# Starting x tile 0 and wk chunk 0 alone on two DMA queues, holding back the other loads, and turning the gate column with a full-height matmul

## The chip, the cores and the metric

The kernel runs on one core of one Trainium2 chip. The metric is the time of one execution in device microseconds (us). Most executions of a kernel agree within some tenths of a per cent, so a kernel is given by the median of several. The profile of an execution spans about 1.3 us less than its time.

Five engines matter. PE is the matrix engine (PEld is its weight load), DVE, ACT and POOL are the vector, the scalar and the GpSimd engine, and SP here only issues transfers. Loads are issued from the queues of SP and ACT (SPq and ACTq) and carried out by 16 DMA engines.

## The reference, cut to what matters

The kernel computes a linear-attention block and a gated feed-forward block on the same input and mixes them with a per-row gate. Only the very beginning matters here: the K and Q projections of the first two of sixteen row tiles of x, and the gate column.

```python
# x: (1, 2048, 640) bf16; wqkv: (640, 1920); gate_w: (640,)
g   = sigmoid((x * gate_w).sum(-1, keepdims=True))
qkv = x @ wqkv                    # q, k, v; 32 heads of 20
pq, pk = phi(q), phi(k)           # phi(t) = where(t > 0, t + 1, exp(t)) + 1e-6
a   = linear_attention(pq, pk, v) @ wo
b   = (gelu(x @ w_gate) * (x @ w_up)) @ w_down
out = g * a + (1 - g) * b
```

## The kernel before

The contraction dimension of 640 is cut into five chunks of 128. `T` transposes a tile of x on PE, `KM(n, ks)` adds the K projection of tile n over the chunks ks, as a 512-wide and a 128-wide matmul for each chunk, and `QM` does the same for Q. `gate_w` becomes column 640 of the Q weights, so that the Q projection also yields the gate; for that it has to be turned from a row into a column. `warm` runs filler matmuls on constants, whose result nobody reads: they are meant to keep PE busy while it waits for data, so that its clock rises early. In the profile below, PE starts a wide matmul every 0.43 us at first (called the cold pace here) and works at twice that pace (warm) from 6.16 us on.

The loads of the opening, in order of issue (`touch` is a small load whose data nobody uses):

```python
P.op("act", lambda e: e.dma_start(touch[0:16, 0:4], A_wqkv[0:128:8, 640:644]), ...)
load_x(0)              # SP queue; each of these is 160 KB
load_wk(0)             # SP
load_x(1, "act")       # ACT
load_wk(1)             # SP
load_wk(3)             # SP
# ... (an activation that loads the Exp table)
load_wk(2, "act")
load_wk(4, "act")
dma_in(gw_sb[0:5, :], gate_w.rearrange("(k p) -> k p", p=128), [r_gw], eng="act")
load_wq(0, 2)          # SP, 320 KB
load_wq(2, KC, "act")  # 480 KB
# ... DMA transposes of tiles 2 to 15, once wk chunk 4 has landed; then all other loads
```

The matmuls of the opening:

```python
def gate_col():
    P.op("pe", lambda e: e.transpose(psb[:, 7, 0:5], gw_sb[0:5, :], ident[0:5, 0:5]), ...)
    P.op("dve", lambda e: e.tensor_copy(wq[:, :, 640:641],
                                        psb[:, 7, 0:5].rearrange("p (k o) -> p k o", o=1)), ...)

warm(5, 512)
warm(1, 128)
T(0, [0], 7)
T(0, [1, 2, 3, 4], 6)
warm(6, 128)
KM(0, [0])
T(1, [0], 7)
T(1, [1, 2, 3, 4], 6)
warm(3, 128)
KM(1, [0])
for k in (1, 3):
    KM(0, [k])
    KM(1, [k])
gate_col()
for k in (2, 4):
    KM(0, [k])
    KM(1, [k])
# ... QM(2), QM(3): the Q projections of tiles 0 and 1; then KQ(i) for tiles 2 to 15; then the rest
```

PE takes these strictly in this order. If one of them waits for a load, everything behind it waits too.

Of the kernel before, what the change touches and what calls it, by code (L numbers as in the profile page):

```python
# [7 lines left out]
BF16 = mybir.dt.bfloat16  # L8
# [152 lines left out]
def bass_gated_mix__linear_attn_block__geglu_ffn__prompt_kernel(  # L161
# [17 lines left out]
    def take(n):  # L179
        nonlocal off  # L180
        o = off
        off += (n + 15) // 16 * 16
        return o
# [35 lines left out]
    O_G = take(32)  # L219
    O_OMG = take(32)  # L220
    O_GW = take(128)
    O_TOUCH = take(16)
    TOTAL = off

    omg_dram = nc.dram_tensor("omg_row", (S,), F32).ap()
# [3 lines left out]
    with (  # L229
# [8 lines left out]
        with contextlib.ExitStack() as stack:  # L238
            dma_sems = [stack.enter_context(nc.semaphore("s_in%d" % i)) for i in range(n_dma_in)]

            P = _Plan(["pe", "act", "dve", "pool", "sp"])
# [9 lines left out]
            def new_dma_key():  # L251
                k = "in%d" % dma_next[0]
                dma_next[0] += 1
                return k

            def v16(o, n):
                return pool[:, o:o + n]
# [5 lines left out]
            psb = ps[:].bitcast(BF16)  # L263


            x_aug = v16(R_XN, NT * XW).rearrange("p (i w) -> p i w", i=NT)
# [4 lines left out]
            wk = wkq[:, :, 0:640]  # L271
            wq = wkq[:, :, 640:1281]
# [23 lines left out]
            ident = v16(O_IDENT, 128)  # L296
# [6 lines left out]
            gg = v32(O_G, 16)  # L303
            omg = v32(O_OMG, 16)
            gw_sb = v16(O_GW, 128)
            touch = v16(O_TOUCH, 16)


            bank = [P.res("bank%d" % b, excl=True) for b in range(8)]
            r_xn = [P.sb("xn%d" % i, R_XN + i * XW, R_XN + (i + 1) * XW) for i in range(NT)]  # L310
# [4 lines left out]
            r_wk = [P.sb("wk%d" % k, R_WK + k * WW, R_WK + k * WW + 640) for k in range(KC)]  # L315
# [27 lines left out]
            r_gw = P.res("gw")  # L343

            def dma_in(dst, src, writes, reads=(), eng="sp"):
                P.op(eng, lambda e, dst=dst, src=src: e.dma_start(dst, src),
                     reads=reads, writes=writes, dma=new_dma_key())



            def load_x(i, eng):
                dma_in(x_aug[:, i, 0:640], A_x[0, i * 128:(i + 1) * 128, :], [r_xn[i]], eng=eng)

            def load_wk(k, eng):
                dma_in(wk[:, k, :], A_wqkv[k * 128:(k + 1) * 128, 640:1280], [r_wk[k]], eng=eng)


            def load_x(i, eng="sp"):
                dma_in(x_aug[:, i, 0:640], A_x[0, i * 128:(i + 1) * 128, :], [r_xn[i]], eng=eng)

            def load_wk(k, eng="sp"):
                dma_in(wk[:, k, :], A_wqkv[k * 128:(k + 1) * 128, 640:1280], [r_wk[k]], eng=eng)

            def load_wq(k0, k1, eng="sp"):
                dma_in(wq[:, k0:k1, 0:640],
                       A_wqkv[k0 * 128:k1 * 128, 0:640].rearrange("(k p) w -> p k w", p=128),
                       r_wq[k0:k1], eng=eng)


            P.op("act", lambda e: e.dma_start(touch[0:16, 0:4], A_wqkv[0:128:8, 640:644]),  # L370
                 writes=[P.res("touch")], dma=new_dma_key())
            load_x(0)
            load_wk(0)
            load_x(1, "act")
            load_wk(1)
            load_wk(3)

            zero = nc.const_aps.tensor(0.0, (128, 1), F32)
            P.op("act", lambda e: e.activation(eg[:, 0:1], zero, ACT.Exp), writes=[r_eg[0]])
            load_wk(2, "act")  # L380
            load_wk(4, "act")
            dma_in(gw_sb[0:5, :], gate_w.rearrange("(k p) -> k p", p=128), [r_gw], eng="act")
            load_wq(0, 2)
            load_wq(2, KC, "act")
# [15 lines left out]
            for c in range(NHC):  # L400
# [9 lines left out]
                 reads=[r_ones], writes=[r_ident])  # L410

            def late_constants():
                P.op("pool", lambda e: e.memset(x_aug[:, :, 640:641], 1.0), writes=[r_xone])
                P.op("pool", lambda e: e.memset(mask, 1.0), writes=[r_mask])
                for lo, hi, base, pat in ((0, 600, 0, [[0, 5], [20, 6], [0, 20]]),
# [5 lines left out]
                    P.op("pool", lambda e, lo=lo, hi=hi, base=base, pat=pat: e.affine_select(  # L421
                        mask[:, lo:hi], mask[:, lo:hi], pat, ALU.is_ge, 0.0, base=base + 19,
                        channel_multiplier=-1), reads=[r_mask], writes=[r_mask])

            one_l = nc.const_aps.tensor(1.0, (128, 128), BF16)
            one_r = nc.const_aps.tensor(1.0, (128, 512), BF16)

            def warm(count, n):
                def fn(e):
                    last = None  # L430
                    for w in range(count):
                        last = e.matmul(ps[:, 4, 0:n], one_l, one_r[:, 0:n], start=True, stop=True)  # L432
                    return last
                P.op("pe", fn, writes=[bank[4]])


            SLOTS = [(0, 1), (2, 3), (4, 5), (6, 7)]
# [1 line left out]
            def slot(n):  # L439
                return SLOTS[n % 4]  # L440

            def T(i, ks, tb):
                def fn(e):
                    last = None
                    for n, k in enumerate(ks):
                        last = e.transpose(psb[:, tb, n * 128:(n + 1) * 128],
                                           x_aug[:, i, k * 128:(k + 1) * 128], ident)
                    return last
                P.op("pe", fn, reads=[r_xn[i], r_ident], writes=[bank[tb]])
                P.op("dve", lambda e: e.tensor_copy(  # L450
                    xT[:, ks[0]:ks[-1] + 1, i * 128:(i + 1) * 128],
                    psb[:, tb, 0:len(ks) * 128].rearrange("p (k s) -> p k s", k=len(ks))),
                    reads=[bank[tb]], writes=[r_xTa[i] if ks[0] == 0 else r_xT[i]])
# [4 lines left out]
            def KM(n, ks):  # L458
                i = seq[n][1]
                b0, b1 = slot(n)  # L460

                def fn(e):
                    last = None
                    for k in ks:
                        lhs = xT[:, k, i * 128:(i + 1) * 128]
                        e.matmul(ps[:, b0, :], lhs, wk[:, k, 0:512], start=(k == 0), stop=(k == KC - 1))  # L466
                        last = e.matmul(ps[:, b1, 0:128], lhs, wk[:, k, 512:640],
                                        start=(k == 0), stop=(k == KC - 1))
                    return last
                P.op("pe", fn, reads=[r_xTa[i] if i < NXN and ks == [0] else r_xT[i]] + [r_wk[k] for k in ks],  # L470
                     writes=[bank[b0], bank[b1]])
# [35 lines left out]
                    reads=[bank[b0], bank[b1], r_e[m]], writes=[r_dst])  # L507

            def gate_col():
                P.op("pe", lambda e: e.transpose(psb[:, 7, 0:5], gw_sb[0:5, :], ident[0:5, 0:5]),  # L510
                     reads=[r_gw, r_ident], writes=[bank[7]])
                P.op("dve", lambda e: e.tensor_copy(wq[:, :, 640:641],
                                                    psb[:, 7, 0:5].rearrange("p (k o) -> p k o", o=1)),
                     reads=[bank[7]], writes=[r_gcol])


            ALLK = list(range(KC))
            warm(5, 512)
            warm(1, 128)
            T(0, [0], 7)  # L520
            T(0, [1, 2, 3, 4], 6)
            warm(6, 128)
            KM(0, [0])
            T(1, [0], 7)
            T(1, [1, 2, 3, 4], 6)
            warm(3, 128)
            KM(1, [0])
            for k in (1, 3):
                KM(0, [k])
                KM(1, [k])  # L530
            gate_col()
            for k in (2, 4):
                KM(0, [k])
                KM(1, [k])
            for n in range(4):
                if n == 2:
                    for k in range(3):
# [42 lines left out]
            for i in range(2, NT):  # L580
                KQ(i)
                if i == 4:
                    late_constants()
            P.op("dve", lambda e: e.tensor_scalar(gg, eg, 0.5, 0.5, ALU.mult, ALU.add),
                 reads=r_eg, writes=[r_g])
            P.op("dve", lambda e: e.tensor_scalar(omg, eg, -0.5, 0.5, ALU.mult, ALU.add),
                 reads=r_eg, writes=[r_omg])
            P.op("sp", lambda e: e.dma_start(omg_dram.rearrange("(i p) -> p i", p=128), omg,
                                             allow_slow_non_contiguous=True),
                 reads=[r_omg], writes=[r_od], dma=new_dma_key())  # L590
# [19 lines left out]
            def ME(g):  # L610
# [17 lines left out]
                for c in cs:  # L628
# [10 lines left out]
                 reads=r_z5, writes=[r_zd], dma=new_dma_key())  # L639
# [310 lines left out]
```

## Time and profile before

| | us |
|---|---|
| time, median of the first 3 executions (range) | 274.76 (274.43 to 275.19) |
| PE busy, of a span of 273.4 | 269.3 |
| first transposes of tile 0 | 3.10 |
| first K projection matmul (tile 0) | 4.38 |
| transposes of tile 1 | 4.87 |
| first Q projection matmul | 8.54 |

From the page of the profile, its summary line, busy times (share of the span, number of instructions) and the chain of work that ended last:

```profile
span 273.4 us, 3515 instructions
...
PE 269.3 (98%) x1385; PEld 130.8 (48%) x1412; DVE 138.9 (51%) x233; ACT 79.1 (29%) x137; POOL 36.2 (13%) x36
...
PE 97%; DVE 1%; issue 1%; ACT 1%; DVEq 0%; ACTq 0%
...
```

PE bounds the kernel. Fillers count as busy, so the busy share does not tell what the opening is worth; the time at which the first Q matmul starts does.

From the timeline of the first 9 us (start in us, duration in us, engine, source line, operation, operands, number of merged instructions; in brackets the idle time before it and what ended that). L432 is a filler, L446 a transpose of x, L466 and L467 the wide and narrow K matmul, L510 the gate column, L481 a Q matmul:

```profile
...
start us, us, engine line op out<-in xcount [idle before <-releaser]
...
0.80 0.40 SPq L346 DMA_DIRECT2D pool<-in_A_x_dram  x1
...
0.84 2.40 PE L432 MATMUL ps<-const-bfloat16-1.0 128*128 128x512 bf16 x6 [0.84 <-PEq L935]
...
1.24 0.45 ACTq L346 DMA_DIRECT2D pool<-in_A_x_dram  x1
1.26 1.83 SPq L346 DMA_DIRECT2D pool<-in_A_wqkv_dram  x4
...
3.10 0.72 PE L446 MATMUL ps<-pool 128*128 128x128 bf16 x5
...
4.38 0.59 PE L466 MATMUL ps<-pool 128*128 128x512 bf16 x1
...
4.87 0.74 PE L446 MATMUL ps<-pool 128*128 128x128 bf16 x5
...
5.41 0.53 PE L432 MATMUL ps<-const-bfloat16-1.0 128*128 128x128 bf16 x3
...
7.19 0.22 PE L467 MATMUL ps<-pool 128*128 128x128 bf16 x1
...
7.34 0.17 PE L510 MATMUL ps<-pool 5*128 5x5 bf16 x1
...
7.45 0.39 PE L466 MATMUL ps<-pool 128*128 128x512 bf16 x1
...
8.54 0.38 PE L481 MATMUL ps<-pool 128*128 128x512 bf16 x1
...
```

Tile 0 was issued at 0.80 us and its transposes start at 3.10, just as the six fillers end. Tile 1 was issued at 1.24 and its transposes start at 4.87, with no idle time in front. A wide and a narrow matmul take about 0.5 us together at the cold pace (4.38 to 4.87) and 0.27 at the warm one (the two pairs between 8.00 and 8.54); the first wide matmul at the warm pace starts at 6.16. Around the gate column, the pair at 7.45 comes 0.20 us later than the narrow matmul at 7.19 and its 0.05 us would have allowed.

Two more views: first, the table of windows, here two stretches of it. The last figure of a line is what the 16 DMA engines moved:

```profile
...
core 0: us, PE busy (x) PEld busy (x) DVE busy (x) ACT busy (x) POOL busy (x), PEclk, DMA share, GB/s
...
3.10:4.60 1.50, 1.50 (x14) 1.23 (x13) 0.65 (x2) 0.12 (x1) 1.30 (x3) 1.00 1.02 360
4.60:6.10 1.50, 1.50 (x11) 1.11 (x10) 0.65 (x2) 0.00 (x0) 0.00 (x0) 1.00 1.01 337
...
```

Second, the list of DMA issues in a short window, with the time from issue to landing. This is the load of x tile 1:

```profile
...
issues: line engine op xcount, KB each, median us to landing
pool<-in_A_x_dram ACTq DMA_DIRECT2D x1, 160.0 KB, 3.2
```

It was issued at 1.24 us and took 3.2 us, so it landed at about 4.4.

### The profile page before, as it was taken

To read this page: it belongs to the slowest core of one execution; us is meant where nothing else is said; L and a number is where in the kernel's file an instruction comes from. 1 tells how busy PE (TensorE), PEld (TensorE's weight loads), DVE (VectorE), ACT (ScalarE), POOL (GpSimd) and SP (SyncE) were. 2 spreads that over 40 slices of the span, in tenths; PEclk is the share of its full clock that TensorE was granted. 3 is DMA by queue.
4 is the path that set the end of the run, shared out by engine and by line. 5 is a ranking of instruction groups with operands and counts; after the bars stand their busy time and mean duration, and the time that the engine had idled before them with its cause. 6 is when DMAs were issued, how large, how long until landed. Compare 5 with 4: busy or idle time off the path is not lost.

```text
span 273.4 us, 3515 instructions
## 1 busy us (share of the span) xinstructions
PE 269.3 (98%) x1385; PEld 130.8 (48%) x1412; DVE 138.9 (51%) x233; ACT 79.1 (29%) x137; POOL 36.2 (13%) x36
## 2 busy tenths in 40 slices
PE   8999999999999999999999999999999999999997
PEld 5555555555445444444444444444444444444444
DVE  1688989610334334999999999534100132222232
ACT  2455555210521453223222223224566100000000
POOL 5000000000000401242332422000000240007000
DMA  7876999511140111612121421390000023111311
GB/s 224 177 106 123 353 401 382 111 26 24 27 48 4 66 52 48 189 38 48 25 48 28 46 48 26 58 314 15 1 0 2 0 58 97 39 38 37 100 38 58
DMA packets 43599, 24.10 MB, mean 88 GB/s; under 512 B 32831, under 2 KB 42047, under 8 KB 43455
## 3 DMA queue, kind: packets, MB, share of 16 engines
q1 hardware_dynamic: 42709, 22.89, 32.2%
q10 hardware_dynamic: 874, 0.98, 1.0%
q8 instruction: 11, 0.18, 0.3%
q14 instruction: 5, 0.04, 0.0%
HBM read 14.16 MB, written 2.63 MB: 61 GB/s over the span
## 4 chain that ended last, share of the span: by engine, by line
PE 97%; DVE 1%; issue 1%; ACT 1%; DVEq 0%; ACTq 0%
PE ps L692 41%; PE ps L885 16%; PE ps L553 12%; PE ps L807 6%; PE ps L602 6%; PE ps L859 4%; PE ps L604 2%; PE ps L670 2%; PE ps L820 2%; PE ps L432 1%; PE ps L466 1%; PE ps L840 1%; PE ps L481 1%; PE ps L713 1%; DVE pool L572 1%
## 5 line engine op out<-in xcount | busy, mean ns | idle before, releaser
L692 PE MATMUL ps<-pool 128*128 128x512 bf16 x510 | 113.0, 379 | 0.5
L692 PEld LDWEIGHTS ps<-pool 128*128 128x128 bf16 x520 | 50.5, 98 | 59.9
L700 DVE TENSOR_TENSOR pool<-ps,pool 128x512 bf16<-128x512 f32 x52 | 35.8, 688 | 33.3 <-PE ps L692 30.2
L698 ACT ACTIVATE pool<-ps 128x512 f32<-128x512 f32 x52 | 31.0, 597 | 72.4 <-PE ps L692 72.4
L885 PE MATMUL ps<-pool 128*128 128x512 bf16 (+2 forms) x217 | 45.4, 366 | 0.2
L746 POOL TENSOR_TENSOR pool<-pool 128x640 f32<-128x640 bf16 x16 | 22.5, 1408 | 138.6 <-DMA pool<-z_row 86.3
L553 PE MATMUL ps<-pool 128*128 128x512 bf16 (+1 forms) x206 | 37.9, 343 | 0.2
L885 PEld LDWEIGHTS ps<-pool 128*128 128x128 bf16 x221 | 21.0, 98 | 24.2 <-issue 0.6
L891 DVE SCALAR_TENSOR_TENSOR pool<-ps,pool 128x512 bf16<-128x512 f32 (+2 forms) x17 | 12.2, 720 | 33.7 <-PE ps L885 33.6
L553 PEld LDWEIGHTS ps<-pool 128*128 128x128 bf16 x210 | 20.5, 98 | 17.5
L572 DVE SCALAR_TENSOR_TENSOR pool<-ps,pool 128x128 bf16<-128x128 f32 (+2 forms) x42 | 25.3, 603 | 2.4
L563 ACT ACTIVATE pool<-ps 128x640 bf16<-128x640 f32 x28 | 19.7, 703 | 18.2 <-DVE pool L572 10.9
L754 DVE TENSOR_TENSOR pool<-pool 128x640 bf16<-128x640 bf16 x16 | 23.1, 1442 | 0.6
L602 PE MATMUL ps<-pool 128*128 128x512 bf16 x77 | 21.4, 379 | 0.0
L864 DVE TENSOR_TENSOR pool<-ps,pool 128x512 f32<-128x512 f32 x4 | 2.8, 692 | 31.0 <-PE ps L859 31.0
L807 PE MATMUL ps<-pool 128*128 128x512 bf16 x80 | 17.9, 379 | 0.0
L604 PE MATMUL ps<-pool 128*128 128x129 bf16 x80 | 17.6, 220 | 0.2
L866 POOL TENSOR_TENSOR pool<-pool 128x512 f32<-128x512 f32 x4 | 5.1, 1264 | 75.7 <-DVE pool L864 75.7
L748 DVE TENSOR_REDUCE pool<-pool 128x32 f32<-128x640 f32 x16 | 12.9, 809 | 0.0
L811 ACT ACTIVATE pool<-ps,pool 128x512 f32<-128x512 f32 x16 | 11.0, 687 | 6.6 <-PE ps L807 6.6
L807 PEld LDWEIGHTS ps<-pool 128*128 128x128 bf16 x80 | 7.8, 98 | 9.4
L602 PEld LDWEIGHTS ps<-pool 128*128 128x128 bf16 x80 | 7.8, 98 | 9.3
(66 smaller groups left out, 130.8 us busy)
## 6 DMA issues: line engine op xcount, KB each, us to landing
out_dram<-pool SPq DMA_DIRECT2D x19, 128.0 KB, 1.8
pool<-in_B_w_gate_dram SPq DMA_DIRECT2D x1, 2080.0 KB, 13.4
pool<-in_B_w_up_dram SPq DMA_DIRECT2D x1, 2080.0 KB, 19.1
pool<-in_A_x_dram SPq DMA_DIRECT2D x1, 1280.0 KB, 8.8
pool<-in_B_w_down_dram SPq DMA_DIRECT2D x1, 1120.0 KB, 7.3
pool<-omg_row SPq DMA_DIRECT2D x1, 1024.0 KB, 5.0
pool<-in_A_x_dram SPq DMA_DIRECT2D x1, 960.0 KB, 5.9
pool<-in_A_wo_dram SPq DMA_DIRECT2D x6, 160.0 KB, 10.4
```

The source lines that it names most:

```text
L553: last = e.matmul(ps[:, b + p, 0:c1 - c0], xT[:, k, i * 128:(i + 1) * 128], wkq[:, k, c0:c1], start=(k == 0), stop=(k == KC - 1))
L563: P.op("act", lambda e: e.activation(e_buf[m], ps_flat[:, o:o + 640], ACT.Exp), reads=banks, writes=[r_e[m]])
L572: P.op("dve", lambda e, c0=c0, c1=c1: e.scalar_tensor_tensor(dst[:, c0:c1], ps_flat[:, o + c0:o + c1], 1.0 + EPS, e_buf[m][:, c0:c1], ALU. ...
L602: e.matmul(ps[:, bs[n], :], lhs, x_aug[:, i, 0:512], start=(i == 0), stop=(i == NT - 1))
L604: last = e.matmul(ps[:, bt, n * 129:(n + 1) * 129], lhs, x_aug[:, i, 512:641], start=(i == 0 and n == 0), stop=(i == NT - 1), skip_group_c ...
L692: last = e.matmul(ps[:, b, :], w[:, k, fc * 128:(fc + 1) * 128], xT[:, k, j * 512:(j + 1) * 512], start=(k == 0), stop=(k == KC - 1))
L698: P.op("act", lambda e: e.activation(ge[n], ps[:, gb, :], ACT.Gelu_apprx_tanh), reads=[bank[gb]], writes=[r_ge[n]])
L700: P.op("dve", lambda e: e.tensor_tensor(hT[fc][:, j * 512:(j + 1) * 512], ps[:, ub, :], ge[n], ALU.mult), reads=[bank[ub], r_ge[n]], write ...
L746: P.op("pool", lambda e: e.tensor_tensor(tmp[n], pq[i], z_b, ALU.mult), reads=[r_pq[i], r_zb], writes=[r_tmp[n]])
L754: P.op("dve", lambda e: e.tensor_tensor(pq[i].rearrange("p (h d) -> p h d", h=32), pq[i].rearrange("p (h d) -> p h d", h=32), den[n].unsqu ...
L807: last = e.matmul(ps[:, b, :], pqnT[:, m, i * 128:(i + 1) * 128], w2[:, m, 0:512], start=(m == 0), stop=(m == KC - 1))
L885: last = e.matmul(ps[:, pb, 0:c1 - c0], hT[fc][:, i * 128:(i + 1) * 128], wd[:, fc, c0:c1], start=False, stop=(fc == NFC - 2), skip_group_ ...
```

## The change

Its intent: let the two loads that the first projection needs have the DMA engines to themselves, so that they land early; drop the touch load; hold x tile 1 and wk chunk 1 back until two wide fillers are done (the "gate" or "tick" below, not to be confused with the gate column); use wk chunk 1, which should then come in time, where three fillers stood; and turn the gate column by a matmul over 128 rows, 123 of them zero, instead of a 5-row transpose.

```diff
-            P.op("act", lambda e: e.dma_start(touch[0:16, 0:4], A_wqkv[0:128:8, 640:644]), ...)
+            r_tick = P.res("tick")
+            warm(2, 512, [r_tick])
             load_x(0)
-            load_wk(0)
-            load_x(1, "act")
-            load_wk(1)
+            load_wk(0, "act")
+            load_wk(1, after=[r_tick])
+            load_x(1, "act", after=[r_tick])
             load_wk(3)
 # ...
+            P.op("dve", lambda e: e.memset(gw_sb, 0.0), writes=[r_gw])
             dma_in(gw_sb[0:5, :], gate_w.rearrange("(k p) -> k p", p=128), [r_gw], eng="act")
 # ... in gate_col:
-                P.op("pe", lambda e: e.transpose(psb[:, 7, 0:5], gw_sb[0:5, :], ident[0:5, 0:5]),
+                P.op("pe", lambda e: e.matmul(ps[:, 7, 0:5], gw_sb, ident[:, 0:5], start=True, stop=True),
 # ... the matmuls:
-            warm(5, 512)
-            warm(1, 128)
+            warm(4, 512)
             T(0, [0], 7)
             T(0, [1, 2, 3, 4], 6)
-            warm(6, 128)
+            warm(4, 128)
             KM(0, [0])
             T(1, [0], 7)
             T(1, [1, 2, 3, 4], 6)
-            warm(3, 128)
+            KM(0, [1])
             KM(1, [0])
-            for k in (1, 3):
+            KM(1, [1])
+            for k in (3, 2):
                 KM(0, [k])
                 KM(1, [k])
             gate_col()
-            for k in (2, 4):
-                KM(0, [k])
-                KM(1, [k])
+            KM(0, [4])
+            KM(1, [4])
```

More of the change, by code (lines that the diff above doesn't have):

```diff
@@ L221, in bass_gated_mix__linear_attn_block__geglu_ffn__prompt_kernel @@
     O_GW = take(128)
-    O_TOUCH = take(16)
     TOTAL = off
@@ L305, in bass_gated_mix__linear_attn_block__geglu_ffn__prompt_kernel @@
             gw_sb = v16(O_GW, 128)
-            touch = v16(O_TOUCH, 16)
             bank = [P.res("bank%d" % b, excl=True) for b in range(8)]
@@ L347, in dma_in, with warm, fn, load_x @@
                      reads=reads, writes=writes, dma=new_dma_key())
-            def load_x(i, eng):
-                dma_in(x_aug[:, i, 0:640], A_x[0, i * 128:(i + 1) * 128, :], [r_xn[i]], eng=eng)
-            def load_wk(k, eng):
-                dma_in(wk[:, k, :], A_wqkv[k * 128:(k + 1) * 128, 640:1280], [r_wk[k]], eng=eng)
-            def load_x(i, eng="sp"):
-                dma_in(x_aug[:, i, 0:640], A_x[0, i * 128:(i + 1) * 128, :], [r_xn[i]], eng=eng)
-            def load_wk(k, eng="sp"):
-                dma_in(wk[:, k, :], A_wqkv[k * 128:(k + 1) * 128, 640:1280], [r_wk[k]], eng=eng)
+            one_l = nc.const_aps.tensor(1.0, (128, 128), BF16)
+            one_r = nc.const_aps.tensor(1.0, (128, 512), BF16)
+            def warm(count, n, tick=()):
+                def fn(e):
+                    last = None
+                    for w in range(count):
+                        last = e.matmul(ps[:, 4, 0:n], one_l, one_r[:, 0:n], start=True, stop=True)
+                    return last
+                P.op("pe", fn, writes=[bank[4]] + list(tick))
+            r_tick = P.res("tick")
+            warm(2, 512, [r_tick])
+            def load_x(i, eng="sp", after=()):
+                dma_in(x_aug[:, i, 0:640], A_x[0, i * 128:(i + 1) * 128, :], [r_xn[i]], reads=after, eng=eng)
+            def load_wk(k, eng="sp", after=()):
+                dma_in(wk[:, k, :], A_wqkv[k * 128:(k + 1) * 128, 640:1280], [r_wk[k]], reads=after, eng=eng)
             def load_wq(k0, k1, eng="sp"):
@@ L367, in load_wq @@
                        r_wq[k0:k1], eng=eng)
-            P.op("act", lambda e: e.dma_start(touch[0:16, 0:4], A_wqkv[0:128:8, 640:644]),
-                 writes=[P.res("touch")], dma=new_dma_key())
             load_x(0)
-            load_wk(0)
-            load_x(1, "act")
-            load_wk(1)
+            load_wk(0, "act")
+            load_wk(1, after=[r_tick])
+            load_x(1, "act", after=[r_tick])
             load_wk(3)
@@ L423, in late_constants @@
                         channel_multiplier=-1), reads=[r_mask], writes=[r_mask])
-            one_l = nc.const_aps.tensor(1.0, (128, 128), BF16)
-            one_r = nc.const_aps.tensor(1.0, (128, 512), BF16)
-            def warm(count, n):
-                def fn(e):
-                    last = None
-                    for w in range(count):
-                        last = e.matmul(ps[:, 4, 0:n], one_l, one_r[:, 0:n], start=True, stop=True)
-                    return last
-                P.op("pe", fn, writes=[bank[4]])
             SLOTS = [(0, 1), (2, 3), (4, 5), (6, 7)]
@@ L509, in gate_col @@
             def gate_col():
-                P.op("pe", lambda e: e.transpose(psb[:, 7, 0:5], gw_sb[0:5, :], ident[0:5, 0:5]),
+                P.op("pe", lambda e: e.matmul(ps[:, 7, 0:5], gw_sb, ident[:, 0:5], start=True, stop=True),
                      reads=[r_gw, r_ident], writes=[bank[7]])
-                P.op("dve", lambda e: e.tensor_copy(wq[:, :, 640:641],
-                                                    psb[:, 7, 0:5].rearrange("p (k o) -> p k o", o=1)),
+                P.op("dve", lambda e: e.tensor_copy(wq[:, :, 640:641], ps[:, 7, 0:5].unsqueeze(2)),
                      reads=[bank[7]], writes=[r_gcol])
             ALLK = list(range(KC))
-            warm(5, 512)
-            warm(1, 128)
+            warm(4, 512)
             T(0, [0], 7)
             T(0, [1, 2, 3, 4], 6)
-            warm(6, 128)
+            warm(4, 128)
             KM(0, [0])
```

## The prediction

> **What bounds it now.** The matrix engine: 269.3 of 273.4 us busy (page, first part), 97% of the chain of waits. After the opening it hardly pauses (2.75 of 2.80 us busy from 8.5 to 11.3, 60.33 of 60.70 from 11.3 to 72, table of windows), so the change can only win by letting useful matmuls begin earlier, and that should reach the end nearly whole. Filler counts as busy; the measure is the start of the first Q matmul, 8.54 us in the timeline.
>
> **The opening, from the timeline.** Fillers run from 0.84, one 512-wide every 0.43 us, the cold pace (the Trainium skill, "TensorE: Matmul & The Clock Gate", Part 1, has 426.7 ns cold, 215.7 warm; the trace agrees: warm 512+128 pairs every 0.27 us). x tile 0, issued at 0.80, lands 2.3 us later; its transposes start at 3.10. wk chunk 0, issued at 1.26, lands 3.0 us later (4.26); the first projection starts at 4.38. Tile 1 transposes at 4.87, three fillers follow (0.32 us), then tile 1's first projection at 5.73. The clock turns warm near 6.04 (estimate: the 512 matmul at 5.73 took 0.37 us). Then K pairs run back to back, except for about 0.2 us around the 5-row gate transpose: the next pair starts at 7.45, not 7.25.
>
> **What the change does.**
> 1. x0 and wk0 start together. wk0 is issued 0.46 us earlier and should land near 3.4. Both share the same 16 engines ("DMA: Bandwidth & Descriptors", Issuing engines are not separate DMA queues), so x0 should land later, at 3.3 to 3.5 (160 KB more at some 350 GB/s is up to 0.45 us). Filler before the transposes grows from 5.25 to 6 units of 0.427: first transpose at 3.40.
> 2. The fillers after it shrink from six to four: first projection near 4.37, unchanged. wk0's lead is spent on x0's delay.
> 3. Tile 1's transposes stay near 4.9; the three fillers behind them become KM(0, k=1). Gain 0.3 us.
> 4. Full-height gate matmul: gains about 0.13 of the 0.2 us.
> 5. Gated loads (wk1, x1) are issued near 1.95 instead of 1.7 and 1.24; later ones shift 0.1 to 0.6 us. Before, they land at 5.3 (wk1), 4.44 (x1), 6.26 (wk4), 8.2 and 8.9 (wq). The engines moved only about 100 GB/s between 2.7 and 3.1 us, 340 to 380 later: flow binds, so I expect wk4 within 0.3 us of before and no wait on wk. wq is tight, needed near 8.1 and 9.2: minus 0.1 us.
>
> The removed touch load (0.41 us of ACT's queue) and the memset on an idle engine are off the chain.
>
> Sum: 0.3 + 0.13 - 0.1, about 0.35 us: first Q matmul near 8.2, total **274.4 us**, about 0.13%, within the spread of three runs (274.43 to 275.19). Range **273.7 to 275.0**. Chances: faster by over 2% 0.01, within 2% 0.98, slower 0.01.
>
> **What would show it.** Right: first transpose near 3.4, first projection near 4.4, no filler after tile 1's transposes, no gap around the gate matmul, first Q matmul at 8.1 to 8.3, everything after it shifted alike. Step 1 wrong: x0 lands at 3.1 or as late as 3.8. Step 5 wrong: weight loads wait for a DMA before KM k=1, k=2 or the Q matmuls.
>
> **What would make it wrong.** The clock turning warm at another time: each us of cold costs half a us of work. x0 or wk1 landing late enough to idle the PE. wq landing after 8.2. Or the lead being eaten where vector work and matmuls alternate (chain of waits, 13.6 to 17.1 us).

## The result, and the profile after

| | before | after |
|---|---|---|
| median of 6 executions | 275.05 | 276.06 (276.00 without the slow one) |
| all executions | 274.43 to 275.51 | 274.92, 275.84, 276.00, 276.13, 276.50, and one of 1634.85 |
| ratio of the fast executions | | 1.0032, interval 1.0008 to 1.0056 |

Ratios here and below compare the mean times of fast executions in the same rounds. They are not quite the ratio of the medians quoted beside them, nor always that of the means of all executions listed (e3 below has ratio 0.9990, its means are 274.60 and 274.78). Fast means: not in the slow state; the execution of 1634.85 us is left out. The change cost about 0.9 us (means 275.88 and 275.00), where I had predicted a gain of 0.35.

The execution of 1634.85 us is the one that was profiled. Its timeline shows why it is no use for a comparison:

```profile
...
0.84 8.01 PE L354 MATMUL ps<-const-bfloat16-1.0 128*128 128x512 bf16 x6 [0.84 <-PEq L927]
...
```

Six wide fillers take 8.01 us there, and the weight loads between them come every 1.28 us: a third of the cold pace of 0.43, and it stayed near there to the end. The view of the cores nevertheless gives a granted clock of 1.000:

```profile
...
core 0: 1633.6 us, clock 1.000
...
```

So the readings of "after" come from later executions of the same, unaltered kernel. Five of them gave a usable profile: e1, e14 and e15 to e17. The lines below are from e16, of 275.55 us. (This one lies well inside the 274.92 to 276.90 us of the kernel's 21 fast executions.)

The page, with the first line of shares of the chain by source line (L684 is the feed-forward matmul that was L692):

```profile
span 274.3 us, 3532 instructions
...
PE 270.2 (99%) x1407; PEld 129.7 (47%) x1407; DVE 138.9 (51%) x234; ACT 79.2 (29%) x137; POOL 36.2 (13%) x36
...
PE 97%; DMA 2%; DVE 0%; SPq 0%; issue 0%
PE ps L684 41%; PE ps L877 16%; PE ps L545 14%; PE ps L594 6%; PE ps L799 6%; PE ps L851 4%; DMA pool<-in_A_wqkv_dram 2%; PE ps L596 2%; PE ps L812 2%; PE ps L662 2%; PE ps L832 1%; PE ps L474 1%; PE ps L459 1%; PE ps L705 1%; PE ps L723 0%
...
```

The chain now contains a DMA: 2% of the span goes to a load of a slice of wqkv. The view of the chain in the first 10 us (start, duration, what) shows which:

```profile
...
2.26 5.44 DMA pool<-in_A_wqkv_dram
...
7.75 0.39 PE ps L459
...
```

It is wk chunk 3, behind the held-back chunk 1 in SP's queue: issued at 2.26 us, hardly later than before (about 2.19), but landed at 7.70 instead of about 6.0. (In the profiles without the tick below, e3, e12 and e18, it landed at 6.0 to 6.5; with the loads of before once, in e2, at 7.7.) Tile 1's load is not on this chain, although PE waited longer for it: had tile 1 come in time, PE would have waited for chunk 3 instead.

The timeline of the opening. L354 is a filler, L439 a transpose of x, L459 and L460 the K matmuls, L504 the gate column, L474 a Q matmul:

```profile
...
0.80 0.40 ACTq L344 DMA_DIRECT2D pool<-in_A_wqkv_dram  x1
...
0.80 0.41 SPq L344 DMA_DIRECT2D pool<-in_A_x_dram  x1
...
1.88 1.29 SPq L344 DMA_DIRECT2D pool<-in_A_wqkv_dram  x3
1.89 0.37 ACTq L344 DMA_DIRECT2D pool<-in_A_x_dram  x1
...
3.81 0.72 PE L439 MATMUL ps<-pool 128*128 128x128 bf16 x5 [0.25 <-DMA pool<-in_A_x_dram]
...
4.74 0.45 PE L459 MATMUL ps<-pool 128*128 128x512 bf16 x1
...
6.01 0.45 PE L439 MATMUL ps<-pool 128*128 128x128 bf16 x5 [0.76 <-DMA pool<-in_A_x_dram]
...
7.75 0.39 PE L459 MATMUL ps<-pool 128*128 128x512 bf16 x1 [0.31 <-DMA pool<-in_A_wqkv_dram]
...
8.79 0.22 PE L460 MATMUL ps<-pool 128*128 128x128 bf16 x1
...
8.84 0.17 PE L504 MATMUL ps<-pool 128*128 128x5 bf16 x1
...
8.87 0.38 PE L459 MATMUL ps<-pool 128*128 128x512 bf16 x1
...
9.41 0.38 PE L474 MATMUL ps<-pool 128*128 128x512 bf16 x1
...
```

Tile 0's transposes start at 3.81 instead of 3.10, and only after an idle 0.25 us. Tile 1's start at 6.01 instead of 4.87, after PE stood idle for 0.76 us waiting for x. At 7.75 there is another idle 0.31 us for wk chunk 3, and this is the wait that ends last. The first Q matmul starts at 9.41 instead of 8.54. In the gate column's place everything went as planned: narrow matmul at 8.79, gate column at 8.84, next pair at 8.87.

The view of waits of PE in the first 9 us (who waited for whom: total us, number of times, longest), which for before had only the start of the program, 0.8 us:

```profile
...
engine line waited for: us in total, times, longest us
PE ps L439 <- DMA pool<-in_A_x_dram: 1.0, 2, 0.8
PE ps L354 <- PEq L927: 0.8, 1, 0.8
PE ps L459 <- DMA pool<-in_A_wqkv_dram: 0.3, 1, 0.3
```

The DMA issues at 1.88 us, and the same two stretches of the table of windows:

```profile
...
issues: line engine op xcount, KB each, median us to landing
pool<-in_A_wqkv_dram SPq DMA_DIRECT2D x1, 160.0 KB, 3.9
pool<-in_A_x_dram ACTq DMA_DIRECT2D x1, 160.0 KB, 4.1
```

```profile
...
3.10:4.60 1.50, 1.25 (x10) 0.80 (x9) 0.27 (x2) 0.67 (x2) 1.30 (x3) 1.00 0.87 211
4.60:6.10 1.50, 0.74 (x8) 0.39 (x6) 0.39 (x1) 0.00 (x0) 0.00 (x0) 1.00 0.91 293
...
```

Tile 1 was issued 0.65 us later than before (1.89 against 1.24) and took 4.1 us instead of 3.2, so it landed 1.55 us later, at 6.0. The engines moved 211 GB/s from 3.1 to 4.6 us and 293 from 4.6 to 6.1, against 360 and 337 before. An estimate from these: 0.29 MB less by 6.1 us, or about 0.8 us of transfer at 350 GB/s.

The loss is all in the opening. In each of these profiles I took the starts of a few instructions and subtracted the start of the first Q matmul from the execution's time ("first warm" is the first wide matmul whose successor starts within 0.30 us):

```text
execution               time    T(0)   T(1)   first warm   first Q   time minus first Q
before                 274.68   3.10   4.87      6.16        8.54        266.13
after (e1)             275.18   3.71   6.04      6.33        9.05        266.13
after (e14)            275.19   3.81   6.10      6.39        9.01        266.18
after (e15)            275.52   3.67   6.48      6.77        9.39        266.13
after (e16)            275.55   3.81   6.01      4.74        9.41        266.14
after (e17)            275.74   3.83   5.72      6.67        9.61        266.13
e2  gate column only   275.53   3.10   5.09      6.87        9.37        266.16
e3  no tick            274.95   3.94   5.41      6.41        8.80        266.15
e4  tick on wk1 only   275.59   3.90   5.37      6.38        9.46        266.13
e5  tick on x1 only    276.76   3.83   6.12      9.77       10.61        266.15
e6  before plus tick   277.05   3.15   5.77     10.38       10.93        266.12
e7  tick after one     275.21   3.95   5.00      4.50        9.05        266.15
e10 before's loads     274.60   3.12   5.32      5.62        8.47        266.12
e12 no tick, filled    274.94   3.92   5.05      4.79        8.79        266.15
e13 before, unfilled   274.70   3.15   4.79      5.42        8.59        266.11
```

(e8 and e9 are left out because their traces lack the record of the first wide Q matmul; e18's profile, 275.18 us with the first Q matmul at 9.05, fits too.) The last column is constant to 0.07 us. Whatever happens before the first Q matmul reaches the end in full, in each of these profiles; nothing behind it takes any of it up or adds to it. So the whole question is what ends last in the first ten microseconds.

### The profile page after: what moved, and what is told of

It is laid out like the page before. It is cut to its first block, busy times and chain, and to the rows that moved or that the text cites. A ratio compares the mean times of both kernels' runs of the same rounds, so it can differ in the third digit from the quotient of the medians.

```text
span 1633.6 us, 3532 instructions
## 1 busy us (share of the span) xinstructions
PE 1630.8 (100%) x1407; PEld 441.4 (27%) x1407; DVE 140.9 (9%) x234; ACT 79.3 (5%) x137; POOL 36.1 (2%) x36
## 4 chain that ended last, share of the span: by engine, by line
PE 100%; DVE 0%; issue 0%
PE ps L684 42%; PE ps L877 17%; PE ps L545 14%; PE ps L594 6%; PE ps L799 6%; PE ps L851 4%; PE ps L596 2%; PE ps L812 2%; PE ps L662 2%; PE ps L459 1%; PE ps L474 1%; PE ps L832 1%; PE ps L354 1%; PE ps L705 1%; PE ps L723 0%; PE ps L475 0%
## 5 line engine op out<-in xcount | busy, mean ns | idle before, releaser
L684 PE MATMUL ps<-pool 128*128 128x512 bf16 x520 | 690.5, 1706 | 0.0
L684 PEld LDWEIGHTS ps<-pool 128*128 128x128 bf16 x520 | 167.1, 322 | 507.9 <-issue 507.4
L877 PE MATMUL ps<-pool 128*128 128x512 bf16 (+2 forms) x221 | 275.9, 1626 | 0.0
L545 PE MATMUL ps<-pool 128*128 128x512 bf16 (+1 forms) x210 | 232.1, 1486 | 0.0
L594 PE MATMUL ps<-pool 128*128 128x512 bf16 x80 | 130.8, 1704 | 0.0
L877 PEld LDWEIGHTS ps<-pool 128*128 128x128 bf16 x221 | 70.2, 320 | 205.3 <-issue 204.9
L545 PEld LDWEIGHTS ps<-pool 128*128 128x128 bf16 x210 | 67.3, 321 | 164.7 <-issue 159.5
L799 PE MATMUL ps<-pool 128*128 128x512 bf16 x80 | 107.4, 1704 | 0.0
L692 DVE TENSOR_TENSOR pool<-ps,pool 128x512 bf16<-128x512 f32 x52 | 35.9, 691 | 615.6 <-PE ps L684 615.6
L851 PE MATMUL ps<-pool 128*128 128x512 bf16 x52 | 68.7, 1691 | 0.0
L596 PE MATMUL ps<-pool 128*128 128x129 bf16 x80 | 57.6, 720 | 0.0
L799 PEld LDWEIGHTS ps<-pool 128*128 128x128 bf16 x80 | 26.1, 327 | 79.7 <-issue 79.7
L594 PEld LDWEIGHTS ps<-pool 128*128 128x128 bf16 x80 | 26.0, 325 | 79.2 <-issue 78.8
L851 PEld LDWEIGHTS ps<-pool 128*128 128x128 bf16 x52 | 15.6, 303 | 53.0 <-issue 53.0
L812 PE MATMUL ps<-pool 128*128 128x512 bf16 x20 | 28.4, 1726 | 0.0
L662 PE MATMUL ps<-pool 128*128 128x512 bf16 x20 | 26.8, 1700 | 0.0
L596 PEld LDWEIGHTS ps<-pool 128*128 128x128 bf16 x80 | 25.6, 320 | 3.7 <-issue 0.4
L561 DVE TENSOR_SCALAR pool<-pool 128x640 bf16<-128x640 bf16 x28 | 9.1, 327 | 194.9 <-ACT pool L555 194.9
```

Source lines behind the costliest of these rows:

```text
L545: last = e.matmul(ps[:, b + p, 0:c1 - c0], xT[:, k, i * 128:(i + 1) * 128], wkq[:, k, c0:c1], start=(k == 0), stop=(k == KC - 1))
L594: e.matmul(ps[:, bs[n], :], lhs, x_aug[:, i, 0:512], start=(i == 0), stop=(i == NT - 1))
L596: last = e.matmul(ps[:, bt, n * 129:(n + 1) * 129], lhs, x_aug[:, i, 512:641], start=(i == 0 and n == 0), stop=(i == NT - 1), skip_group_c ...
L662: last = e.matmul(ps[:, b, :], wgu[:, k, :], xT[:, k, j * 512:(j + 1) * 512], start=(k == 0), stop=(k == KC - 1))
L684: last = e.matmul(ps[:, b, :], w[:, k, fc * 128:(fc + 1) * 128], xT[:, k, j * 512:(j + 1) * 512], start=(k == 0), stop=(k == KC - 1))
L692: P.op("dve", lambda e: e.tensor_tensor(hT[fc][:, j * 512:(j + 1) * 512], ps[:, ub, :], ge[n], ALU.mult), reads=[bank[ub], r_ge[n]], write ...
```

## The experiments

All eighteen runs gave correct results; six of them (e1, e11, e14 to e17) are the changed kernel unaltered. Theory A: the tick makes loads late that PE needs next, and PE waits. Theory B: the idle time that this opens also keeps the clock cold for longer. Theory C: the lead is won and lost again later. C fell at once with the table above. Executions in the rounds were not profiled, apart from the first of each kernel.

### e1: the changed kernel again, unaltered

> The changed kernel unaltered, to get a profile in the fast state: the one on record ran every 512-wide matmul in about 1.28 us or more and cannot be read beside before. Theory A (late loads): about 0.9 us slower than before, with weight-load idle put down to a DMA of x tile 1, wk or wq in the opening, and the first Q matmul near 9.4 us instead of 8.54. Rival B (clock): no DMA wait, but the 512-wide matmuls stay at the 0.43 us pace for about 1.5 us longer. Rival C (the lead is lost later): first Q matmul near 8.2, and the loss between there and the end. If the 1.6 ms execution belongs to the kernel it comes again.

Measured: ratio 1.0031 (1.0018 to 1.0043), median 275.76. Tile 1's transposes waited 0.82 us for x and started at 6.04; the first Q matmul started at 9.05; no 1.6 ms execution came. The slowdown is reproduced and A's wait is there. This profile fell on the fastest of the five executions, in which the clock was already warm before the wait.

### e2: only the gate column

```diff
 # kernel before
+            P.op("dve", lambda e: e.memset(gw_sb, 0.0), writes=[r_gw])
             dma_in(gw_sb[0:5, :], gate_w...)
-                e.transpose(psb[:, 7, 0:5], gw_sb[0:5, :], ident[0:5, 0:5])
+                e.matmul(ps[:, 7, 0:5], gw_sb, ident[:, 0:5], start=True, stop=True)
```

> The kernel before with the full-height gate matmul and the zeroed rows alone. My prediction: 0.1 to 0.15 us faster than before (below what five rounds resolve, so the trace decides): the 0.2 us hole around the gate matmul falls to under 0.1 us. Rival: the hole is not from the 5-row shape and stays near 0.2 us.

Measured: ratio 1.0001 (0.9987 to 1.0015), no difference in time that five rounds can resolve. The hole in the trace is nearly gone: narrow matmul at 8.20, gate column at 8.26, next pair at 8.28, where the 0.20 us had been lost. The same three lines from the timeline of e10, which has the same gate column:

```profile
...
7.62 0.22 PE L468 MATMUL ps<-pool 128*128 128x128 bf16 x1
7.68 0.17 PE L511 MATMUL ps<-pool 128*128 128x5 bf16 x1
7.71 0.38 PE L467 MATMUL ps<-pool 128*128 128x512 bf16 x1
```

The narrow matmul streams for 0.05 us, so the pair at 7.71 is about 0.03 us late. The 5-row transpose had cost the rest (the edit changes the height and also replaces the transpose by an ordinary matmul; which of the two matters was not separated). Note also that in this profile, with the loads of before, wk chunk 1 landed at 6.8 us instead of 5.3 and the execution took 275.53: the landings of one and the same sequence of loads vary by more than a microsecond between executions (wk chunk 3 of the unaltered changed kernel landed between 6.7 us in e1 and 7.9 in e17).

### e3: no tick

```diff
 # changed kernel
-            load_wk(1, after=[r_tick])
-            load_x(1, "act", after=[r_tick])
+            load_wk(1)
+            load_x(1, "act")
```

> The changed kernel without the gate on the two fillers: wk chunk 1 and x tile 1 are issued as soon as the queue is free (near 1.2 us instead of 1.95). Theory A: the gating costs the time, so this is about 0.9 us faster than the changed kernel and 0 to 0.4 us faster than before; x tile 1 and wk chunk 1 land 0.4 to 0.7 us earlier. Rivals B and C: within 0.3 us of the changed kernel.

Measured: ratio 0.9990 (0.9976 to 1.0004), median 274.75. In the same rounds the changed kernel's mean is 275.64 and this one's 274.60: the tick alone costs 1.03 us, more than the whole slowdown. Tile 1 landed at 4.8 us and its transposes started at 5.41 with no wait. This is the main result; the next four runs ask how the tick does it.

### e4 and e5: the tick on one of the two loads

```diff
 # e4, changed kernel                                # e5, changed kernel
-            load_x(1, "act", after=[r_tick])        -            load_wk(1, after=[r_tick])
+            load_x(1, "act")                        +            load_wk(1)
```

> The changed kernel with the gate left on wk chunk 1 and taken off x tile 1. Theory A1 (the gate costs because x tile 1 comes late and its transposes are next in the matmul queue): x tile 1 lands near 4.8 us, its transposes start near 5.0 to 5.4 instead of 6.04, most of the 1.1 us comes back (ratio to before 1.000 to 1.001), unless KM k=1 then waits for wk chunk 1 (landed at 5.8 us in the gated run), which would leave 0.2 to 0.4 us. Rival A2 (wk chunk 1 and what queues behind it matters): ratio stays at 1.003.

> The mirror: the gate left on x tile 1 alone. Theory A1: nothing comes back, ratio 1.0025 to 1.004, transposes of tile 1 still start near 6 us. Rival A2: ratio near 0.999 to 1.000.

Measured: e4 has ratio 1.0015 (1.0001 to 1.0028), e5 1.0078 (1.0065 to 1.0091). With x tile 1 free, about half of the loss remains. Its transposes start at 5.37 in the profile, and the first use of wk chunk 1 then waits 0.31 us, in the place foreseen. But that wait is not the one that ended last in this profile: the first Q matmul itself waited 0.35 us for its slice of wq, which was issued at 2.74 us and landed at 9.33, and so would have started at 9.46 in any case. With only x tile 1 held back, all five executions took 276.6 us or more, worse than with both held back. That I had not expected (the changed kernel itself was not in these rounds). The timeline of e5 shows PE idle for 0.62 us for x, and then the cold pace for more than three microseconds (L459 is a wide K matmul; the first at the warm pace is the one at 9.77):

```profile
...
6.12 0.71 PE L439 MATMUL ps<-pool 128*128 128x128 bf16 x5 [0.62 <-DMA pool<-in_A_x_dram]
6.63 0.63 PE L459 MATMUL ps<-pool 128*128 128x512 bf16 x1
...
9.77 0.38 PE L459 MATMUL ps<-pool 128*128 128x512 bf16 x1
...
```

So holding back x tile 1 costs more than holding back wk chunk 1 (A), and idle time can coincide with a much later warm clock (B).

### e6: the tick alone, on the kernel before

```diff
 # kernel before
+            warm(2, 512, [r_tick])      # two of its five wide fillers, moved up
-            load_x(1, "act")
-            load_wk(1)
+            load_x(1, "act", after=[r_tick])
+            load_wk(1, after=[r_tick])
-            warm(5, 512)
+            warm(3, 512)
```

> The kernel before, with nothing of the change but the gate: x tile 1 and wk chunk 1 wait for two of its five wide fillers (touch load, queues, order and gate column as before). Theory A: slower than before by 0.4 to 1.0 us, ratio 1.0015 to 1.0035, with a new wait of tile 1's transposes for x. Rival D (the gate only hurts together with wk chunk 0 at the head of the second queue): within 0.1% of before.

Measured: ratio 1.0026 (1.0006 to 1.0045), median 275.36. The tick needs nothing else of the change to do harm: tile 1's transposes waited 0.74 us and started at 5.77. The profiled execution is the slowest of the six (277.05 us) and was again cold to 10.38 us; the others took 274.99 to 275.48, by their mean 0.42 us more than before.

### e7: the tick after one filler instead of two

```diff
 # changed kernel
-            warm(2, 512, [r_tick])
+            warm(1, 512, [r_tick])
 # ...
-            warm(4, 512)
+            warm(5, 512)
```

> The changed kernel with the gate opening after one filler instead of two, so 0.43 us earlier (issue near 1.46 instead of 1.89 us), all else alike. Theory A: the cost of the gate follows its length: 0.3 to 0.6 us faster than the changed kernel, ratio 1.001 to 1.002. Rival E (any gate costs, by stalling the two issuing queues or by the semaphore): ratio stays at 1.003.

Measured: ratio 1.0001 (0.9989 to 1.0013). Releasing the two loads 0.43 us earlier took away not half of the loss but all of it. In the profile the wait for tile 1 is gone: it landed at 4.96 us, and PE, which was ready for it at 4.95, began its transposes at 5.00. This fits A: what counts is whether a load makes the moment at which PE asks for it, not how long it was held back. But the profile is of the slowest of the five executions (275.21 us); in it PE waited 0.37 and 0.44 us for wk chunks 3 and 4 instead, and the first Q matmul (9.05) came no earlier than e1's. What ended last in the four faster ones was not seen. The rival, that any such gate costs by stalling the issuing queues, falls by the ratio.

### e8 and e9: the idle time filled

```diff
 # e8: changed kernel; e9: the same on e5
             KM(0, [0])
+            warm(8, 128)
             T(1, [0], 7)
```

> The changed kernel with eight 128-wide fillers (0.85 us at the cold pace) put in front of tile 1's transposes, so that the matmul engine does not stand idle while it waits for x tile 1. No load and no useful matmul moves earlier. Theory B (the idle gap also postpones the warm clock, and that is the larger part of the loss in the slower executions): 0.3 to 0.7 us faster than the changed kernel in the median, ratio 1.000 to 1.002, and the 512-wide matmuls are warm by about 7.3 us in the profile. Theory A alone (only the wait for x counts): no change, or up to 0.1 us slower.

> The kernel with the gate on x tile 1 alone, in which all five executions took 276.6 us or more and the clock stayed cold to 9.8 us in the profile, with the same eight fillers before tile 1's transposes. Theory B: 1.2 to 1.9 us faster than that kernel (275.0 to 275.5 us, ratio 1.001 to 1.003), warm before 7.5 us. Theory A alone: stays at 276.6 or above.

Measured: e8 has ratio 1.0030 (1.0018 to 1.0042), as the changed kernel. B's forecast failed there. In e8's profile (276.23 us, its slowest execution) the clock is warm by the time of the projections, but the next thing in line, wk chunk 3, arrives late, and the wait of 0.81 us at 8.43 takes up everything:

```profile
...
6.18 0.48 PE L439 MATMUL ps<-pool 128*128 128x128 bf16 x5
6.50 0.38 PE L459 MATMUL ps<-pool 128*128 128x512 bf16 x1
...
8.43 0.39 PE L459 MATMUL ps<-pool 128*128 128x512 bf16 x1 [0.81 <-DMA pool<-in_A_wqkv_dram]
...
```

In e9 the ratio fell from 1.0078 to 1.0045 (1.0028 to 1.0063): means 276.95 and 276.13, on different chips and rounds. That is 0.8 us of the 1.2 to 1.9 that B had forecast, and the profile was warm by 6.82 us. This fits a cold clock as a part of e5's loss, though with one profile of each kernel it is not shown for all five executions; for the changed kernel's usual loss, e8 speaks against it.

### e10: the loads of before, with the other two parts of the change

```diff
 # e2, that is before with the new gate column
-            warm(3, 128)
+            KM(0, [1])
             KM(1, [0])
-            for k in (1, 3):
+            KM(1, [1])
+            for k in (3, 2):
 # ... and KM(0, [4]), KM(1, [4]) behind the gate column, as in the changed kernel
```

> The load program of before (touch load, x tile 0 and wk chunk 0 on one queue, no gate) with the full-height gate column and the changed order of projections (KM k=1 in place of the three fillers). What I predicted for these two parts: first Q matmul 0.3 to 0.4 us earlier than before, ratio 0.9985 to 0.9995. Rival (the projections only catch up with loads that land at 5.3 to 6.8 us for wk chunk 1, so an idle gap opens): no gain, ratio 1.000 to 1.002.

Measured: ratio 1.0008 (0.9990 to 1.0027), inconclusive: five executions of 274.60 to 275.08 and one of 276.30. In the profile, the first Q matmul starts at 8.47, only 0.07 us earlier than before's. That execution had an idle wait of 0.35 us for wk chunk 0, as large as what is missing of the predicted gain.

### e13: idle time without late loads

```diff
 # kernel before
-            warm(6, 128)      # between tile 0's transposes and KM(0, [0])
-            warm(3, 128)      # after tile 1's transposes
```

> The kernel before with its nine narrow fillers taken out (six after tile 0's transposes, three after tile 1's): no load and no useful matmul has a new wait, the matmul engine only stands idle for about 0.6 and 0.3 us where it ran fillers. Theory B (an idle stretch by itself postpones the warm clock): 0.5 to 1.7 us slower than before, ratio 1.002 to 1.006, warm only after 7 us in the profile. Theory A alone (only waits for data cost): within 0.2 us of before.

Measured: ratio 1.0015 (0.9990 to 1.0040), and a clear split: 274.46, 274.60, 274.67 and 274.70, but also 275.95 and 276.53. Most executions do not mind the idle time; two lost 1.5 to 2 us. The profiled one was among the quick four and warm at 5.42, so the cause in the slow two was not seen. It fits B as an occasional event; e5 and e6 show what such an execution looks like. It does not explain a shift of the median.

### e11, e14 to e17: what ends last in a usual execution of the changed kernel

> The changed kernel unaltered once more, as the control on this chip and for a second profile in the fast state. Ratio 1.002 to 1.004. If the profiled execution takes 275.7 us or more, theory B expects the 512-wide matmuls cold after the wait for x tile 1 (past 6.3 us); theory A alone expects them warm by 6.3 us and a longer wait for x.

> The changed kernel unaltered again. For the clock: a second fast profile; if that execution takes 275.6 us or more I expect the loads of wk (chunk 3 or 2) or the clock, not x tile 1 alone, to be what ends last before the first Q matmul, as in the filled variant, where 0.81 us of waiting for wk chunk 3 took the place of the idle time. For the execution of 1.6 ms: two of seventeen executions so far; if it is tied to this kernel, about one in three profiled executions shows it again.

> A look at the changed kernel, to catch an execution of 275.5 us or more in a profile; the two fast profiles so far were both 275.2 us, with the clock warm near 5 us, before the wait for x tile 1. Theory B expects an execution of 276 us or more to be cold after that wait (first warm 512-wide matmul after 7 us); theory A expects it warm by 6.4 us and held by a load of wk or wq.

> As the look before it: what ends last before the first Q matmul in an execution of 275.5 us or more, the clock (theory B) or a load (theory A). Total minus the start of the first Q matmul should again be 266.1 us.

> As the look before it. With three looks I also expect one execution of 1.6 ms if that state is tied to this kernel, and none if it was chance.

Measured: e11 has ratio 1.0032 (1.0020 to 1.0045) for its fast executions; its profiled execution took 1634.67 us and is again unusable. e14 has 1.0033 (1.0014 to 1.0051) with a profile of 275.19. The three looks took 275.52, 275.55 and 275.74, close to 275.75, the median of the 21 fast executions and these three; none was of 1.6 ms. In these three, PE is at the warm pace by 6.8 us at the latest, and it is loads that PE waits for: tile 1 (1.12 us of idle time) in e15; tile 1 (0.76) and wk chunk 3 (0.31) in e16, shown above; tile 1 (0.22) and wk chunk 3 (0.54) in e17. By the chain, the wait that ends last is tile 1's in e15, and in e1 and e14, but wk chunk 3's in e16 and e17, where it landed at 7.70 and 7.89. So in the usual execution it is A, not B, and the load that counts is tile 1 in some and wk chunk 3 in others. Note also e15: PE was at the cold pace before its wait of 1.12 us and at the warm pace right after it, so idle time does not always keep the clock cold.

### e12 and e18: no tick, and one more filler

```diff
 # e3, that is the changed kernel without its tick
-            warm(4, 512)
+            warm(5, 512)      # PE had idled 0.38 us there
```

> The candidate for beating both: the changed kernel without the gate, with five wide fillers before tile 0's transposes instead of four, so the matmul engine does not idle for the 0.38 us in which it waited there. Ratio 0.9975 to 0.9995 (0.1 to 0.7 us faster than before) if the idle stretch mattered there too; 0.999 to 1.000 if not.

> The best candidate again (no gate, five wide fillers before tile 0's transposes), because the ungated kernels came out at 0.9990 and 0.9992 with intervals that reach 1.0004. If the ungated part of the change is worth the 0.2 to 0.3 us that the two runs suggest, the ratio is 0.998 to 0.9998 again; if it is worth nothing, it scatters to 1.000 or above.

Measured: 0.9992 (0.9980 to 1.0004), median 274.56 against 274.81; and on another draw of chip 0.9967 (0.9942 to 0.9992), median 274.36 against 275.14, where before itself had two executions above 276.5. No version did better, but the first run does not tell this one from e3 (0.9990). The gain is 0.25 us by the first run's means (274.60 against 274.85), and only the second run's interval excludes zero; there the means differ by 0.93 us, and by 0.59 without the two slow executions of before. In e18's profile (275.18 us, the slowest of its six) the gate column itself waited 0.55 us for the load of `gate_w`, a load that no run here varied.

## Why the prediction was wrong

Right:

- The bound and the bookkeeping. A microsecond won or lost in the opening is a microsecond of the total; the time after the first Q matmul was 266.11 to 266.18 us everywhere.
- The gate column (step 4). The hole of 0.20 us shrank to 0.03 where `gate_w` was there in time (e2, e10, e14 to e17); in e1, e3 and e18 the matmul waited for that load.
- Sharing (step 1), in kind. With wk chunk 0 beside it, tile 0 landed 2.8 to 3.1 us after its issue instead of 2.3. I had said 3.3 to 3.5 us on the clock; it was 3.6 to 3.9, and the transposes of tile 0 started at 3.67 to 3.83 instead of the predicted 3.40, which is a second, smaller miss. The Trainium skill ("DMA: Bandwidth & Descriptors", Issuing engines are not separate DMA queues) says that the two queues share the same 16 engines, and this trace agrees: the second queue did not keep tile 0 at its old time.

Wrong:

- **Steps 3 and 5, the step that failed.** I wrote "Tile 1's transposes stay near 4.9" and, of the loads behind the tick, "flow binds, so I expect wk4 within 0.3 us of before and no wait on wk". Tile 1's transposes started between 5.72 and 6.48 in five profiles, after 0.22 to 1.12 us of idle PE; wk chunk 4 landed at about 8.8 us in e16 against 6.26 before (most of this is not the tick's: without it chunk 4 landed at 8.0 to 8.2 in e3, e12 and e18, and with the loads of before at 6.2 to 6.4 in e10 and e13, but 7.9 in e2); and PE waited for wk chunk 3 in two, where this wait, and not tile 1's, ended last. I had the issue time right (1.95 predicted, 1.89 measured) and knew tile 1's landing before (4.44), but never put the two together: with the old 3.2 us from issue to landing, 1.95 gives 5.15, already later than the 4.9 at which I let its transposes start. In fact the time from issue to landing grew too, to between 3.8 and 4.5 us. (Even without the tick the 4.9 was out of reach: in e3, where tile 1 landed at 4.8, its transposes started at 5.41, behind the late tile 0.)
- The reason behind step 5. I took the transfer rate after 3.1 us as fixed and concluded that a later start would be caught up. In e16 the engines moved 211 GB/s in the stretch from 3.1 to 4.6 us, where before had 360, and 293 against 337 in the next. But e3, without the tick, moved 366 and then only 219: by 6.1 us it was 0.17 MB behind before (an estimate from these rates), against 0.29 MB in e16. So only a part of the lag is the tick's. That the held-back issues left the engines without work is not shown; their busy share in e16's first stretch was 0.87.
- In the sum: predicted 0.3 + 0.13 - 0.1 = a gain of 0.35 us; measured a loss of 0.88. The tick, which I had charged with 0.1 us, costs 1.03 (e1 against e3 in the same rounds). Without it the change gains 0.2 (e3) to 0.25 us (e12, with one more filler) by the means, somewhat less than the 0.43 that I had counted for the other two terms, and no single one of these two runs excludes zero. So one term of the sum was mis-sized by a factor of ten, and the rest was of the right sign and order.
- The range. I gave it the spread of before. A kernel that waits for loads in the opening can also take over the scatter of those loads: the 21 fast executions of the changed kernel range over 2 us. Those of before stayed within 1.1 us in five of its sets, though the set beside e18 reached 277.13.

Open:

- Why the engines run at about 100 to 270 GB/s for one to two microseconds in the openings of the changed kernel. With the tick that stretch begins at 3.0 to 3.25 us (five profiles) and falls on tile 1 and wk chunk 1. With the tick 0.43 us earlier (e7) it begins near 4.25, without it (e3) near 4.75, when these two have landed or nearly so. So the tick moves it, but why it comes at all is not explained.
- Why e5, with one load held back, is worse than the change with both.
- Whether the executions of 1.6 ms belong to this kernel. Two of its 26 executions were such, and none of some 120 of the others. With two events this may be chance.

## What to carry to other kernels

When a change holds back a load, put two numbers side by side before anything else: issue time plus the measured time from issue to landing, and the moment at which the in-order engine asks for that data; a load that misses it costs the wait, unless a later load would have ended later anyway, and everything queued behind it on the same queue moves as well. So the longest wait is not always the one that counts: follow the chain to the one that ends last. Loads issued early in a kernel should not be held back to give others room unless the trace shows that the held-back ones have slack. And where an interval of the opening reaches the end in full, compare the start of the first steady-state instruction across profiles: it explained each profiled execution's time here to 0.07 us, where whole times differed by only some tenths of a per cent.

## What the Trainium skill lacked or had wrong

- "TensorE: Matmul & The Clock Gate", Part 1 ("K is binary"), knows the half and the full clock (and 13/16 of it under a current limit) and, in a caveat, a clock stuck at a quarter for over 50 us. Two executions here ran wide matmuls every 1.28 us, a third of the cold pace of 0.43, for 1.6 ms, from the first to the last, and the granted clock that the profile reports was 1.000 throughout.
- The same page, Part 1, puts the warm-up at about 3.4 us of sustained activity and says that it varies with the phase of a free-running window. It does not say what a short idle stretch within the ramp can cost. Here, after 0.62 us (e5) and 0.74 us (e6) of idle PE around 5.5 us, the first warm wide matmul came at 9.77 and 10.38 us, against 6.16 in before; after 0.80 us of idle time in e14, with the clock already rising, it did not matter, nor after 1.12 us in e15, where the pace before had still been cold. What decides between these cases no run here shows.
- The same page, Part 4, says that the full clock does not engage for PE transposes. Five transposes (which the profile lists as MATMUL) took 0.71 us (cold) and 0.45 us (once PE was warm, e16), and the matmul behind them started 0.50 and 0.29 us after the first of them, so they do run at the faster pace when it has been granted; whether they help to earn it, no run here shows.
- "DMA: Bandwidth & Descriptors", Anatomy of one DMA, fits a transfer's time as 2.0 us plus bytes over 436 GB/s, for another issuing path than the one used here; for 160 KB that gives an estimate of 2.4 us. Tile 0 with only the touch load of 0.1 KB beside it took 2.2 to 2.3, beside wk chunk 0 2.8 to 3.1, and tile 1 behind another load 3.1 to 3.7, or 3.8 to 4.6 when held back by 0.65 us. The fit has no term for what else is in flight.
- "TensorEngine Tiling (Array Packing)", Key Properties, says that changing the tiling mode drains the engine, but gives no cost. Around a 5-row transpose between full-height matmuls 0.20 us were lost here, around the full-height matmul over zeroed rows 0.03; that a mode change is the cause fits, but no run separates it from the transpose as such.
